# Fetching a 768-word vector as six rows and turning it on TensorE, and loading ScalarE's root table at another place, in a fused attention and gated feed-forward kernel

## The chip, the cores and the metric

The kernel runs on one core of a Trainium2 chip. The time is device microseconds of one execution; before the change the median of four runs is 443.28 us (442.66 to 444.04). A core has five engines, each with its own queue of instructions that it works off in order: TensorE (PE, matmuls; its weight loads, PEld, overlap them), VectorE (DVE), ScalarE (ACT), GpSimd (POOL) and SyncE (SP). They wait for one another by semaphores. DMAs are issued from the queues of SP, ACT and POOL and carried out by 16 DMA engines. ACT evaluates functions from tables; before a function whose table set is not the active one stands an instruction that loads it, ACT_TABLE_LOAD.

## The reference

Eight batches, twelve heads, 448 positions, heads 64 wide. Attention with a squared relu in place of a softmax, then a root-mean-square norm and a gated feed-forward part:

```python
scores = scale * np.matmul(q, k.transpose(0, 1, 3, 2))      # q, k, v: (8, 12, 448, 64) f32
attn = np.maximum(scores, 0.0) ** 2 / S
x = np.matmul(attn, v)                                      # -> (3584, 768)
rms = np.sqrt(np.mean(x * x, axis=-1, keepdims=True) + 1e-06)
xn = x / rms * rms_g                                        # rms_g: (768,)
g = xn @ w_gate                                             # (768, 1536)
silu = g * (1.0 / (1.0 + np.exp(-g)))
return silu * (xn @ w_val) @ w_out                          # (1536, 768), out (3584, 768) f32
```

## The kernel before, in words

Everything is computed in bf16 with f32 sums, one batch at a time, and transposed: x of a batch, `xT`, has the model dimension on the 128 partitions, in six pieces (`KT` = 6) of 448 columns. The norm's weights g must therefore be a column per piece: `ga_sb`, 128 x 6, in which word kt*128 + p of g stands at partition p, column kt, times a constant. `ga_sb` is read wherever a batch's attention output leaves PSUM for `xT` (function `leave`, line 329, on ACT, two pieces at a time; lines 322 and 337 for two pieces of batch 0).

**The order** is the program's order; nothing reorders it. Each engine gets its instructions in the order in which the Python code emits them. `weave` merges a main list (gate and value projections, then output projection tiles) with a list of side steps (attention of the next batch, its norm, fetches), each with a position in the main list.

**The start.** SP fetches the first two heads of k (line 633), ACT those of q, then SP fetches g (line 635) straight into columns. POOL issues the rest. DVE casts the first k (line 648), ACT the first q (649), and DVE makes `ga_sb` from g (line 651). Meanwhile PE does twelve matmuls on zeros (`warm(12)`, line 663). Then the units of `attention_first(0)` follow: unit 0 is `pe_transposes(0, 0)`, sixteen transposes of 112 x 64 into PSUM (line 143), copied out by DVE (line 149); unit 1 is `scores` (line 187), whose relus go to ACT (197) and DVE (195).

**PSUM** has four buffers in the pool `ps_m` (tag "mm"), taken in turn, and two larger ones in `ps_s`.

**The end of a batch's attention.** For batches 1 to 7 the attention output leaves in three pairs of pieces. `leave` of the last pair (pieces 4 and 5) is a side step after the last gate and value block of the batch before; for batches 2 to 7 ACT does two squares (294) and two scaled copies (329) in it, for batch 1 the copies and then one square. Then come two output projection tiles (one for batch 1), whose PSUM ACT copies to `ost` (line 587) and whose store SP issues (602). Then `norm_stat` sums the squares on PE (461), takes the root on ACT (465), loads Silu's table by a one-column Silu (470), takes the reciprocal on DVE (471), spreads it to all partitions (486 on DVE, 488 on ACT), and `norm_apply` multiplies the six pieces by it on DVE (500). After each pair of pieces `swap` copies the halves of the partitions crosswise into `xD` by two DMAs on SP (342). The gate and value projections (`rounds`, line 520) read six pieces of `xT` and six of `xD`, each as a pair of half-height matmuls into psG and psV. Relu, copies and squares between the Silus and the root ask for no table load.

Of the kernel before, what the change touches and what calls it, by code (L numbers as in the profile page):

```python
# [8 lines left out]
FP32 = mybir.dt.float32  # L9
BF16 = mybir.dt.bfloat16  # L10
ALU = mybir.AluOpType
ACT = mybir.ActivationFunctionType
# [17 lines left out]
def along(p0, gap, fns):  # L30
    return [(p0 + gap * i, f) for i, f in enumerate(fns)]
# [3 lines left out]
def kernel(  # L35
# [11 lines left out]
    nc = tc.nc  # L47
    P = nc.NUM_PARTITIONS
# [5 lines left out]
    KT, FT, HP = DM // P, F // P, H // 2  # L54
    assert HP == KT and (2 * S) % P == 0
    eps = 1e-6
    inv_attn = 1.0 / (float(D) * float(S))
# [5 lines left out]
    def pool(name, bufs=1, **kw):  # L63
        return ctx.enter_context(tc.tile_pool(name=name, bufs=bufs, **kw))

    const = pool("consts")
    wpool = pool("weights")
# [6 lines left out]
    ps_m = pool("ps_m", 4, space=bass.MemoryType.PSUM)  # L74
# [4 lines left out]
    def head_rows(t, b, h0, h1):  # L79
        return t[b, h0:h1].rearrange("h (p c) d -> p h (c d)", c=NCH)  # L80
# [12 lines left out]
    def load(nm, b, h0=0, h1=H):  # L93
        src = {"q": q, "k": k, "v": v}[nm]
        return nc.gpsimd.dma_start(out=ld[nm, b][:, h0:h1, :], in_=head_rows(src, b, h0, h1))
# [192 lines left out]
    def leave(b, js):  # L288

        psAV = psAVs.pop((b, js))  # L290
        last = (b, js[0]) == (0, HP - 1)

        def squares_of(i0, i1, o):
            nc.scalar.activation(out=o, in_=psAV[:, i0:i1, :], func=ACT.Square, scale=inv_attn)

        def square():
            if b < 2:
                squares_of(0, len(js), x2s[b][:, js[0] : js[-1] + 1, :])
                return
            t = sums[b]  # L300
            if js[0] == 0:
                squares_of(0, 2, t[:])
                return
            two = npool.tile([P, 2, S], FP32, name="x2f", tag="x2")
            for i in range(2):
                o = two[:, i, :]
                squares_of(i, i + 1, o)
                if js[0] == 2:
                    nc.vector.tensor_tensor(out=t[:, i, :], in0=t[:, i, :], in1=o, op=ALU.add)
                    if i:  # L310
                        nc.vector.tensor_tensor(
                            out=t[:, 0, :], in0=t[:, 0, :], in1=t[:, 1, :], op=ALU.add
                        )
                else:
                    nc.vector.tensor_tensor(out=t[:, 0, :], in0=t[:, 0, :], in1=o, op=ALU.add)

        if last:
            square()
            low, high, every = slice(0, HALF), slice(HALF, P), slice(0, P)
            j = js[0]  # L320
            for dst, to, fr in ((xTs, every, every), (xDs, low, high), (xDs, high, low)):
                nc.vector.tensor_scalar_mul(
                    out=dst[b][to, j, :], in0=psAV[fr, 0, :], scalar1=ga_sb[fr, j : j + 1]
                )
            return
        if b > 1:
            square()
        for i, j in enumerate(js):
            nc.scalar.mul(out=xTs[b][:, j, :], in_=psAV[:, i, :], mul=ga_sb[:, j : j + 1])  # L329
        if b < 2:  # L330
            square()

    def cross(b, j, psAV):

        low, high = slice(0, HALF), slice(HALF, P)
        for to, fr in ((low, high), (high, low)):
            nc.scalar.mul(out=xDs[b][to, j, :], in_=psAV[fr, 0, :], mul=ga_sb[fr, j : j + 1])
# [190 lines left out]
    def early_out(b, fb, parts):  # L528

        t = late["early"].tile([P, 2, S], FP32, name="gv", tag="gv")  # L530
        for part in range(2):
            nc.scalar.copy(out=t[:, part, :], in_=parts[part][:, :S])
        early[fb] = t
# [96 lines left out]
    with fpool as fp:  # L630
        for nm, src, eng in (("k", k, nc.sync), ("q", q, nc.scalar)):
            first[nm] = fp.tile([PC, 2, NCH * D], FP32, name="first_" + nm, tag="first_" + nm)
            eng.dma_start(out=first[nm][:], in_=head_rows(src, 0, 0, 2))
        g_sb = wpool.tile([P, KT], FP32, name="g_sb", tag="rmsg")
        nc.sync.dma_start(out=g_sb[:], in_=moe_rms_g.rearrange("(kt p) -> p kt", p=P))
        load("k", 0, 2, 4)
        load("q", 0, 2, 4)
        ident = const.tile([PC, PC], BF16, name="ident", tag="ident")
        masks.make_identity(nc, ident[:])
        warm_in = const.tile([P, S], BF16, name="warm_in", tag="warm_in")  # L640
        nc.vector.memset(warm_in[:], 0.0)
        ones_bf = const.tile([P, P], BF16, name="ones_bf", tag="ones_bf")
        nc.vector.memset(ones_bf[:], 1.0)
        eps_col = const.tile([P, 1], FP32, name="eps_col", tag="eps_col")
        nc.vector.memset(eps_col[:], eps)
        warm_act = const.tile([P, 1], FP32, name="warm_act", tag="warm_act")
        nc.scalar.activation(out=warm_act[:], in_=eps_col[:], func=ACT.Sqrt)
        nc.vector.tensor_copy(out=ld["k", 0][:, :2, :], in_=first["k"][:])
        nc.scalar.copy(out=ld["q", 0][:, :2, :], in_=first["q"][:])
    ga_sb = wpool.tile([P, KT], FP32, name="ga_sb", tag="rmsga")  # L650
    nc.vector.tensor_scalar_mul(out=ga_sb[:], in0=g_sb[:], scalar1=inv_attn)
    load("k", 0, 4, 6)
    load("q", 0, 4, 6)
    load("v", 0, 0, 6)
    load("k", 0, 6, 12)
    load("q", 0, 6, 12)
    load("v", 0, 6, 12)

    def warm(n):

        ps = ps_m.tile([P, S], FP32, name="psW", tag="mm")
        for _ in range(n):
            nc.tensor.matmul(out=ps[:], lhsT=warm_in[:, :P], rhs=warm_in[:], start=True, stop=True)  # L663
# [16 lines left out]
    def trans_fill(b, half):  # L680
        transposes(b, half)
        fill(b, half, nc.gpsimd)

    with tc.tile_pool(name="qkT", bufs=2, side="right") as tp, tc.tile_pool(
        name="early", bufs=EB, side="right"
    ) as ep:
        late["qkT"], late["early"] = tp, ep
        warm(12)
        steps = attention_second(1)

        def early_block(fb):
            return [ps_m.tile([P, S], FP32, name="psE", tag="mm")[:] for _ in range(2)]

        units = attention_first(0)
        tail = len(units) - 4
        for n, fn in enumerate(units[:tail]):
            fn()
            if n % 3 == 2 and n < tail - 1:
                warm(2)


        raw_x = xTs[0], xDs[0]
        psSS = ps_m.tile([P, S], FP32, name="psSS", tag="mm")
        blocks = [early_block(0)]

        def part(fb, *rs):
            for r in rs:
                rounds(0, fb, blocks[fb], r, r + 1, raw_x)

        psAV4 = psAVs[0, (HP - 2,)]  # L710
        squares_last, leave_4, attend_5, leave_5 = units[tail:]
        squares_last()
        part(0, *range(HP - 2))
        pe_transposes(1, 0)
        leave_4()
        attend_5()
        leave_5()
        cross(0, HP - 2, psAV4)
        part(0, KT, HP - 2, KT + 1, KT + 2)
        norm_stat(0, psSS, steps.pop(0))  # L720
        norm_spread(0)
        blocks.append(early_block(1))
        part(1, *range(KT))
        part(0, HP - 1)
        part(1, *range(KT, KT + 3))
        part(0, KT + 4)
        steps.pop(0)()
        part(1, KT + 4)
        norm_apply(0)
        for fb in range(2):  # L730
            part(fb, KT + 3, KT + 5)
            early_out(0, fb, blocks[fb])
            if fb == 0:
                pe_transposes(1, 1)
        for fb in range(2, EB):
            blocks.append(early_block(fb))
            for r0 in range(0, 2 * KT, KT):
                steps.pop(0)()
                rounds(0, fb, blocks[fb], r0, r0 + KT, raw_x)
            early_out(0, fb, blocks[fb])  # L740
        main = gate_value(0, EB, KT // 2)
        sides = along(6.4, 2, [lambda fb=fb: early_scale(0, fb) for fb in range(EB)])
        sides += along(10.4, 2, [lambda fb=fb: early_rest(0, fb) for fb in range(EB)])
        sides += along(0, (len(main) - 1) / len(steps), steps[:-1])
        sides += [(26, lambda: trans_fill(2, 0))]
        alloc_ld(2)
        load("q", 2)
        load("k", 2)
        for s in range(4, FT // 2):
            fetch_o(s)  # L750
        sides += [(26, lambda: load("v", 2))]
        weave(main, sides)
# [55 lines left out]
```

## Time and profile before

| what | before |
|---|---|
| median of four runs | 443.28 us |
| the profiled execution | 443.27 us, of which span 441.4 us |
| granted TensorE clock, mean | 0.998 |
| PE busy | 432.5 us, 98% |
| ACT busy | 287.6 us, 65% |
| DVE busy | 289.0 us, 65% |
| table loads before the root (L465) | 7 of 1.28 us, 77.8 to 386.4 |
| table loads before the one-column Silu (L470) | 8 of 1.28 us, 34.5 to 388.1 |
| table load before the one-column root at the start (L647) | 1 of 1.28 us, at 1.2 |
| g's transfer (L635) | issued at 1.18, landed 3.9 us later |
| packets under 512 B in the first 8 us | 880 of 2606 |

A line of a timeline has the start in us from the span's beginning, the duration in us, the engine (PEld is PE's weight load; a q behind the name marks its queue, which issues DMAs), the line of the kernel, the operation, what it writes and reads, shapes, how many instructions are merged, and in brackets how long the engine sat idle before it and what it is thought to have waited for. PE's matmuls are pipelined and their ends are modelled: a matmul is drawn with 0.35 us where one starts every 0.19.

### The profile page before, as it was taken

Reading aid. Unit: us, or ns where it says so; the run is one execution under the profiler, and the core shown is the slowest. Engines: PE = TensorE matmul, PEld = TensorE weight load, DVE = VectorE, ACT = ScalarE, POOL = GpSimd, SP = SyncE. Lnnn points to the kernel's source line nnn. Section 1 sums busy time; section 2 is a strip of 40 time slices with the busy share of each in tenths; the row PEclk is TensorE's granted clock in tenths of the full one; section 3 lists DMA queues with packets and bytes.
Section 4 is the critical chain, followed back from the end, with each engine's and each line's share of the span. In section 5 each row is a group of like instructions: output and inputs, shape, how many; then the busy total and the mean of one; then the engine's idle time right before and its main releaser. Section 6 shows DMA issues by size and latency. Waiting matters only on the chain.

```text
span 441.4 us, 10928 instructions
## 1 busy us (share of the span) xinstructions
PE 432.5 (98%) x4718; PEld 248.9 (56%) x4718; DVE 289.0 (65%) x387; ACT 287.6 (65%) x445; POOL 53.7 (12%) x79
## 2 busy tenths in 40 slices
PE   7999999999999999999999999999999999999996
PEld 3445555655566555655566555655557555665564
DVE  4989985777863867766864668578776468742211
ACT  4899886677685775777755776766766677552220
POOL 8333301030001200021000300003000000000000
PEclk9999999999999999999999999999999999999999
DMA  9999999999216991189904996169913900041013
GB/s 146 196 205 198 201 211 188 177 188 153 57 37 148 212 161 29 37 177 168 167 2 105 194 202 85 37 108 198 175 33 75 214 15 1 1 113 59 1 37 109
DMA packets 87632, 53.21 MB, mean 121 GB/s; under 512 B 36768, under 2 KB 83232, under 8 KB 87584
## 3 DMA queue, kind: packets, MB, share of 16 engines
q0 software_dynamic: 44496, 27.50, 43.3%
q1 hardware_dynamic: 42464, 24.44, 27.8%
q8 instruction: 37, 0.61, 0.5%
q10 hardware_dynamic: 624, 0.57, 0.4%
q14 instruction: 11, 0.09, 0.1%
HBM read 47.19 MB, written 11.01 MB: 132 GB/s over the span
## 4 chain that ended last, share of the span: by engine, by line
PE 86%; ACT 7%; DVE 4%; issue 1%; DMA 1%; SPq 0%; ACTq 0%; DVEq 0%
PE psG L520 30%; PE psO L435 23%; PE psV L520 13%; PE psAV L273 9%; PE psS L228 6%; ACT r L217 2%; PE psW L663 2%; DVE r L240 1%; PE psS L187 1%; ACT r L197 1%; ACT sil L564 1%; DVE hT L566 1%; DVE xT L500 1%; DMA xD<-xT 1%; PE psT L143 1%
## 5 line engine op out<-in xcount | busy, mean ns | idle before, releaser
L520 PEld LDWEIGHTS <-wgv_sb 64*128 64x128 bf16 x2304 | 125.2, 94 | 95.5 <-issue 8.1
L520 PE MATMUL psV<-xD,wgv_sb 64*128 64x448 bf16 x558 | 128.4, 349 | 0.3 <-DMA xD<-xT 0.2
L520 PE MATMUL psG<-xD,wgv_sb 64*128 64x448 bf16 x558 | 128.5, 349 | 0.0
L520 PE MATMUL psG<-xT,wgv_sb 64*128 64x448 bf16 x558 | 128.4, 349 | 0.0
L520 PE MATMUL psV<-xT,wgv_sb 64*128 64x448 bf16 x558 | 128.0, 349 | 0.1
L242 ACT ACTIVATE r<-psS 112x896 bf16<-112x896 f32 x108 | 99.1, 918 | 20.5 <-PE psS L228 17.9
L435 PE MATMUL psO<-wo_sb,hT 128*64 128x512 bf16 (+2 forms) x1368 | 111.8, 323 | 0.0
L566 DVE TENSOR_TENSOR hT<-sil,psV 128x448 bf16<-128x448 bf16 x93 | 57.5, 618 | 62.6 <-ACT sil L564 62.4
L246 DVE TENSOR_TENSOR r<-r 112x1792 bf16<-112x1792 bf16 x72 | 78.0, 1088 | 29.2 <-ACT r L242 28.8
L435 PEld LDWEIGHTS <-hT 128*64 128x64 bf16 x1368 | 74.9, 110 | 35.6 <-issue 0.4
L564 ACT ACTIVATE sil<-psG 128x448 bf16<-128x448 f32 x93 | 50.5, 543 | 58.5 <-PE psV L520 35.5
L228 PE MATMUL psS<-qT,kT 64*128 64x448 bf16 (+1 forms) x288 | 56.1, 350 | 0.4
L587 ACT COPY ost<-psO 128x512 f32<-128x512 f32 (+1 forms) x54 | 25.1, 477 | 39.8 <-PE psO L435 39.8
L273 PE MATMUL psAV<-r,vb 112*64 112x448 bf16 x384 | 40.3, 355 | 0.0
L240 DVE TENSOR_SCALAR r<-psS 112x896 bf16<-112x896 f32 x36 | 39.0, 1084 | 1.8 <-PE psS L228 1.8
L175 POOL DMA_DIRECT2D qT<-qT x12 | 6.5, 542 | 264.0 <-PE psS L228 214.3
L273 PEld LDWEIGHTS <-vb 112*64 112x64 bf16 x384 | 20.1, 109 | 18.5 <-issue 6.5
L329 ACT ACTIVATE xT<-psAV,ga_sb 128x448 bf16<-128x448 f32 x47 | 27.8, 646 | 3.9 <-PE psAV L273 3.8
L228 PEld LDWEIGHTS <-kT 64*128 64x128 bf16 (+1 forms) x288 | 19.0, 97 | 16.0 <-issue 4.7
L500 DVE TENSOR_TENSOR xT<-xT,rstd 128x448 bf16<-128x448 bf16 x48 | 26.4, 618 | 2.3 <-ACT rstd L488 2.3
L471 DVE RECIPROCAL rhalf<-rhalf 128x224 f32<-128x224 f32 x8 | 12.4, 1553 | 21.3 <-ACT rhalf L465 21.3
L256 DVE TENSOR_TENSOR r<-r 112x1792 bf16<-112x1792 bf16 x23 | 24.3, 1082 | 0.7 <-ACT r L217 0.7
(68 smaller groups left out, 279.7 us busy)
## 6 DMA issues: line engine op xcount, KB each, us to landing
vb<-in_v_dram POOLq DMA_DIRECT2D x7, 672.0 KB, 18.1
xD<-xT SPq DMA_DIRECT2D x42, 112.0 KB, 2.3
qb<-in_q_dram POOLq DMA_DIRECT2D x6, 672.0 KB, 11.4
kb<-in_k_dram POOLq DMA_DIRECT2D x6, 672.0 KB, 14.4
qT<-qT POOLq DMA_DIRECT2D x24, 168.0 KB, 3.8
out_dram<-ost SPq DMA_DIRECT2D x7, 336.0 KB, 3.9
wgv_sb<-in_moe_w_gate_dram POOLq DMA_DIRECT2D x6, 384.0 KB, 17.5
wgv_sb<-in_moe_w_val_dram POOLq DMA_DIRECT2D x6, 384.0 KB, 17.4
```

The lines of the kernel that those rows point to most:

```text
L228: nc.tensor.matmul(out=psS[: end - o, hf, :S], lhsT=flat[prt, o:end], rhs=qT[prt, 1 - hf : 3 - hf, h % HH], start=True, stop=True,)
L240: nc.vector.tensor_relu(out=r[:, cp], in_=src)
L242: nc.scalar.activation(out=r[:, cp], in_=src, func=ACT.Relu)
L246: nc.vector.tensor_tensor(out=r[:], in0=r[:], in1=r[:], op=ALU.mult)
L273: nc.tensor.matmul(out=part[hh * D : (hh + 1) * D, :], lhsT=ld["v", b][:, 2 * j + hh, c * D : (c + 1) * D], rhs=rsq[b, 2 * j + hh, c], sta ...
L329: nc.scalar.mul(out=xTs[b][:, j, :], in_=psAV[:, i, :], mul=ga_sb[:, j : j + 1])
L435: nc.tensor.matmul(out=ps[prt, :w], lhsT=lhsT[:, prt], rhs=rhs, start=start, stop=stop)
L500: nc.vector.tensor_tensor(out=x[:, kt, :], in0=raw_x[:, kt, :], in1=rstds[b][:], op=ALU.mult)
L520: nc.tensor.matmul(out=parts[part][:, :S], lhsT=wgv_sb[prt, h, fb * P : (fb + 1) * P], rhs=src[prt, kt, :], start=(r == 0), stop=(r == 2 * ...
L564: nc.scalar.activation(out=s[:], in_=psG, func=ACT.Silu)
L566: nc.vector.tensor_tensor(out=hT[:, fb, o : o + S], in0=s[:], in1=psV, op=ALU.mult)
L587: (nc.vector.tensor_copy if last else nc.scalar.copy)(out=osts[i, t][:, o : o + w], in_=ps[:, :w])
```

## The change

Two edits. First, g is fetched as six rows of 128 words, `g_rows`, a row per partition. A 6 x 6 identity in f32 is copied on DVE from the bf16 one. After unit 0, PE transposes `g_rows` into a PSUM tile 128 x 6 of the "mm" buffers, and DVE scales that into `ga_sb`. The scaling at line 651 is gone. Second, for batches 1 to 7 a one-column root is computed on ACT at the end of `leave` of the last pair; since the active table set is Silu's there, the load of the root's set stands in front of this instruction, and the root in `norm_stat` finds its set active.

```diff
@@ leave
         if b < 2:
             square()
+        if b and js[-1] == HP - 1:
+            nc.scalar.activation(out=warm_act[:], in_=eps_col[:], func=ACT.Sqrt)
@@ the start
-        g_sb = wpool.tile([P, KT], FP32, name="g_sb", tag="rmsg")
-        nc.sync.dma_start(out=g_sb[:], in_=moe_rms_g.rearrange("(kt p) -> p kt", p=P))
+        g_rows = wpool.tile([KT, P], FP32, name="g_rows", tag="rmsg")
+        nc.sync.dma_start(out=g_rows[:], in_=moe_rms_g.rearrange("(kt p) -> kt p", p=P))
...
     ga_sb = wpool.tile([P, KT], FP32, name="ga_sb", tag="rmsga")
-    nc.vector.tensor_scalar_mul(out=ga_sb[:], in0=g_sb[:], scalar1=inv_attn)
+    ident_g = const.tile([KT, KT], FP32, name="ident_g", tag="ident_g")
+    nc.vector.tensor_copy(out=ident_g[:], in_=ident[:KT, :KT])
...
+    def columns_of_g():
+
+        psg = ps_m.tile([P, KT], FP32, name="psg", tag="mm")
+        nc.tensor.transpose(out=psg[:], in_=g_rows[:], identity=ident_g[:])
+        nc.vector.tensor_scalar_mul(out=ga_sb[:], in0=psg[:], scalar1=inv_attn)
...
         for n, fn in enumerate(units[:tail]):
             fn()
+            if n == 0:
+                columns_of_g()
             if n % 3 == 2 and n < tail - 1:
                 warm(2)
```

## The prediction, made before the changed kernel was run

> **What bounds the kernel now.** I read the page first: engine totals, the 40 slices, the chain that ended last.
>
> ```profile
> PE 432.5 (98%) x4718; PEld 248.9 (56%) x4718; DVE 289.0 (65%) x387; ACT 287.6 (65%) x445; POOL 53.7 (12%) x79
> ...
> PE   7999999999999999999999999999999999999996
> ...
> PE 86%; ACT 7%; DVE 4%; issue 1%; DMA 1%; SPq 0%; ACTq 0%; DVEq 0%
> ```
>
> TensorE (PE) works from the first slice to the last, and 86% of the chain is its own matmuls. So a shorter wait on another engine is worth time only where a PE instruction is late today, and whatever holds PE's queue back is paid in full. The rest of the reading is a search for both kinds of place, with the timeline of the two stretches that the edit touches. First the start, all engines:
>
> ```profile
> 1.16 4.66 PE L663 MATMUL psW<-warm_in 128*128 128x448 bf16 x12 [1.16 <-DVE warm_in L641]
> 1.18 0.44 SPq L635 DMA_DIRECT2D g_sb<-in_moe_rms_g_dram  x1
> ...
> 4.31 0.57 DVE L648 CAST kb<-first_k 112x512 bf16<-112x512 f32 x1 [3.06 <-DMA first_k<-in_k_dram]
> ...
> 5.09 0.30 DVE L651 TENSOR_SCALAR ga_sb<-g_sb 128x6 f32<-128x6 f32 x1 [0.21 <-DMA g_sb<-in_moe_rms_g_dram]
> ...
> 5.75 0.37 PEld L143 LDWEIGHTS <-kb 112*64 112x64 bf16 x8 [0.73 <-DVE ga_sb L651]
> ...
> 6.13 0.49 PE L143 MATMUL psT<-ident,qb 112*64 112x112 bf16 x8
> ...
> 6.43 0.69 DVE L149 COPY qkT<-psT 128x448 bf16<-128x448 bf16 x2 [1.04 <-PE psT L143]
> ...
> 7.17 0.56 PE L187 MATMUL psS<-qkT 64*128 64x448 bf16 x4 [0.56 <-DVE qkT L149]
> ...
> 7.77 1.09 DVE L195 TENSOR_SCALAR r<-psS 112x896 bf16<-112x896 f32 x1 [0.65 <-PE psS L187]
> ```
>
> The twelve warming matmuls hold PE until 1.16 + 4.66 = 5.82. Then come sixteen transposes, until 6.13 + 0.49 = 6.62, and then PE waits 0.55 us, to 7.17, for VectorE's (DVE's) two copies. DVE in turn is idle between 7.12 and 7.77.
>
> Next the end of a batch's attention, ScalarE (ACT) alone, where batch 3's x leaves:
>
> ```profile
> 178.45 1.20 ACT L329 ACTIVATE xT<-psAV,ga_sb 128x448 bf16<-128x448 f32 x2
> 179.81 0.59 ACT L587 COPY ost<-psO 128x512 f32<-128x512 f32 x1 [0.16 <-PE psO L435]
> 181.12 0.37 ACT L587 COPY ost<-psO 128x256 f32<-128x256 f32 x1 [0.72 <-PE psO L435]
> 181.50 1.28 ACT L465 ACT_TABLE_LOAD   x1
> 182.80 0.45 ACT L465 ACTIVATE rhalf<-psSS,eps_col 128x224 f32<-128x224 f32 x1
> ```
>
> The load stands in front of the root, and ACT idles 0.16 + 0.72 us ahead of it, waiting for the output projection. Last, PE where it first uses the normed and swapped x, for batch 3 and then for batch 7:
>
> ```profile
> 192.22 0.35 PE L520 MATMUL psG<-xD,wgv_sb 64*128 64x448 bf16 x1
> 192.63 0.35 PE L520 MATMUL psV<-xD,wgv_sb 64*128 64x448 bf16 x1
> ...
> 193.02 0.35 PE L520 MATMUL psG<-xD,wgv_sb 64*128 64x448 bf16 x1
> ...
> 193.57 0.35 PE L520 MATMUL psV<-xD,wgv_sb 64*128 64x448 bf16 x1 [0.20 <-DMA xD<-xT]
> ...
> 396.91 0.35 PE L520 MATMUL psG<-xD,wgv_sb 64*128 64x448 bf16 x1
> 397.24 0.35 PE L520 MATMUL psV<-xD,wgv_sb 64*128 64x448 bf16 x1
> ```
>
> Undisturbed, a psG and a psV start together and the next pair 0.19 us later (189.20, 189.39, 189.58). Steps of 0.41 and 0.55 at batch 3, and of 0.33 at batch 7, are waits for a swap's DMA: 0.22 + 0.36 + 0.14 = 0.72 us. The bracket shows only 0.20 of it, because matmuls are drawn overlapping. I found no such step before the xD of batches 2, 4, 5 or 6.
>
> **The start, part by part.** Removed: the 768-word transfer (0.44 us of SP's queue at 1.18, landed 3.9 us later) and DVE's 0.30 us at 5.09. SP's next instruction is a swap at 16.55, so a shorter issue moves nothing; POOL's queue is not touched. The 768 packets leave the rings while the first k and q land, and those could come earlier; but k's cast ends at 4.88 and q's at 4.88 + 0.62 = 5.50, both before PE is through its warming matmuls at 5.82. The gain is 0.
>
> Added on DVE: a 6x6 copy behind k's cast (the 128x1 memset, 0.06 us, is the nearest row) in the 1.04 us of idle time before 6.43; and the scaling, now read from PSUM, behind the two copies. At L651's 0.30 us it runs 7.12 to 7.42 and L195 is not due before 7.77: 0.35 us to spare, and beyond that L195 waits, and PE's scores behind it. ga_sb is first read at 15.89 (ACT L329).
>
> Added on PE: one fp32 transpose of 6 rows, behind the sixteen. No fp32 matmul is in the trace. From below: the sixteen bf16 ones take 0.03 us each in the chain (0.51 us for 16), so it is hidden. From above: the slowest L143 weight load and matmul, 0.18 + 0.30, with a change of tile form before and after at the 0.37 us that the weight loader shows at such changes, 1.22 us, less the 0.55 us of room: 0.67 us late, with scores and everything behind them on PE. A gain is excluded, since the instruction is new. I take 0, by L143, the same operation. It also needs g on chip: 5.09 today behind 768 packets, with 1.5 us to spare before 6.62. Its PSUM buffer is one more turn of the four "mm" ones; of the tiles after it, the first finds the warming tile, which nobody reads, the next two the copied psT, the fourth itself, read by 7.42.
>
> **The table load, part by part.** Seven batches (1 to 7) get one Sqrt of one column behind the last leave: 7 x 0.20 = 1.4 us more on ACT, 65% busy. The loads stay as many; seven of them move from in front of L465 to in front of the new Sqrt. Between the two places ACT has only copies and squares, for which the trace shows no load.
>
> At batch 3: the leave ends at 178.45 + 1.20 = 179.65; load to 180.94, small root to 181.16. Now both copies are due, and two back to back take 0.84 (the row at 185.54): 182.00. psSS is ready (PE's four L461 end at 181.27), so L465 runs from 182.02 instead of 182.80: 0.78 us earlier. Behind it Silu's load, the reciprocal, the spread, DVE's six L500 and the six swaps follow in the same order, all 0.78 earlier if the DMAs are as long. The last swap landed at 193.53 and would at 192.75; the psV that wants it would, with the earlier 0.22 regained, be due at 192.80. So both steps vanish, and by the same offsets batch 7's: 0.72 us. At batch 1 the order is leave to 76.61, load, small root to 78.10, one copy to 78.71: L465 0.42 us earlier, where no PE step is late.
>
> What is queued behind the moved load: the first copy, from 179.81 to 181.17 (1.36 us later), and the second, some 0.5. A copy frees a PSUM buffer. The first projection tile's is next wanted four tiles on, after psO2, psSS and psO3: 181.27 + 2.6 (two thirds of the 3.92 us for 48 matmuls) = 183.9, against 181.76 when it is free; 2.1 us to spare. Without it, each us of delay would be one of PE. On SP the output store waits for the second copy and is issued 0.5 us later, at 182.0 for 0.79; the swaps behind it, at 186.85 - 0.78 = 186.07, are not reached. No DMA is issued from ACT in between.
>
> One rule speaks against the move. The Trainium skill, ScalarE: Activation LUTs, section "What ACT_TABLE_LOAD costs", puts every switch at about 2.66 us, a drain of some 1.38 included. The trace shows the next activation 1.30 us after the load began (181.50, 182.80), and no drain. By the page the root at batch 3 would start at 179.65 + 2.66 + 0.20 + 0.84 = 183.35, some 0.55 later than today, and that estimate, paid at batches 3 and 7, makes 444.4 us.
>
> **The sum** is made against the profiled execution's own 443.27 us (span 441.4 and 1.87 around it; the median of the runs shown is 443.28): 443.27 - 0.72 + 0 = 442.55. From 57.4 to the end PE shows no other wait above 0.1 us, and its small waits on DVE's relus (0.07 us, six times) hang on PE's own earlier work, so a gain at 193 is kept.
>
> **The rivals.**
> *Nothing to gain at the swaps.* Four of the six comparable batches show no late xD with the same offsets. At batch 3 the last swap's issue held SP 1.37 us instead of 0.57, and its landing took 3.24 us where others' median is 2.2. Batch 5 shows a 1.38 too, unhurt. If that is chance, or follows the swap wherever it goes, 0 to 0.14 is gained: 443.1 to 443.3. Against it: the profiled execution is as long as the median, and an earlier swap helps at any length.
> *The turn of g holds PE (the other side).* The transpose stands in PE's queue ahead of all scores. If g lands late, every 0.1 us past 6.6 costs 0.1. It eats the 0.72 when the transpose ends past 7.9 and makes the kernel slower by 0.9 when past 8.8. The transfers issued in the first 8 us landed after 3.5 to 8.1 us; at 8.1 g comes at 9.3, PE resumes at about 9.5, +2.3 - 0.72: 444.9. Against it: that one is 336 KB on POOL's queue; g is 3 KB and today's slower form needs 3.9.
> *More is gained.* The wait list says that the first weight load waited 0.73 for DVE's ga_sb, which the change takes away. At the warming matmuls' pace it could come at 5.24, 0.51 sooner: 442.04. Against it: that load reads only kb, which was cast at 4.88, and after every warming pair the next form's weights come 0.07 us before the pair's drawn end, as here (5.75, 5.82).
>
> **How the numbers follow.** A measurement of this kernel can tell about 0.2%, 0.89 us, from no change: 442.4 to 444.2 is "same". Swaps gained 0.50; nothing gained 0.25; more gained 0.13; PE held at the start 0.12, of which 0.08 past 444.2. The likeliest, 442.55, is inside the band but 0.16 from its edge, so 0.10 of its share ends beyond: with 0.13 that makes 0.23 faster, 0.08 slower, 0.69 same. The range goes from 442.04 to the nothing-gained case with the transpose's upper bound, 443.27 + 0.67 = 443.94, and 0.15 beyond both for the median's own spread (the runs shown lie 0.6 and 0.8 about theirs): 441.9 to 444.1.
>
> **What would show it.** Right: seven ACT_TABLE_LOADs behind the last leave and none in front of L465; at batch 3 the root at about 182.0; a psG to psV step of 0.19 where 0.41, 0.55 and 0.33 stood; PE's first scores still at 7.17. Wrong: scores later than 7.3, a psO matmul that waits for a copy, a load followed by an idle ACT, or a step of 0.4 still there with the swaps earlier.

## The result and the profile after

The changed kernel takes 442.46 us (median of 37 runs, 441.64 to 443.18) against 443.37 us (58 runs) for the kernel before: a ratio of 0.9979, interval 0.9975 to 0.9984, so 0.7 to 1.1 us faster. The profiled execution took 442.53 us, its span 440.7. The page says little: PE is as busy, its share of the chain that ended last is up from 86% to 89%, and no DMA stands in that chain any more. Nearly all of the 771 packets fewer are g's words.

```profile
PE 432.2 (98%) x4719; PEld 248.9 (56%) x4719; DVE 289.0 (66%) x388; ACT 287.4 (65%) x452; POOL 53.7 (12%) x79
...
DMA packets 86861, 53.22 MB, mean 121 GB/s; under 512 B 35990, under 2 KB 82460, under 8 KB 86812
...
PE 89%; ACT 7%; DVE 3%; issue 1%; DVEq 0%
```

The start, all engines (start, duration, engine, line; lines from 333 on are two or more higher than before):

```profile
1.16 4.66 PE L672 MATMUL psW<-warm_in 128*128 128x448 bf16 x12 [1.16 <-DVE warm_in L643]
...
1.19 0.38 SPq L637 DMA_DIRECT2D g_rows<-in_moe_rms_g_dram  x1
...
4.79 0.15 DVE L654 CAST ident_g<-ident 6x6 f32<-6x6 bf16 x1
...
5.75 0.37 PEld L143 LDWEIGHTS <-kb 112*64 112x64 bf16 x8 [0.73 <-issue]
...
6.64 0.16 PEld L665 LDWEIGHTS psg<-ident_g,g_rows 6*128 6x128 f32 x1
6.64 0.25 PE L665 MATMUL psg<-ident_g,g_rows 6*128 6x6 f32 x1
...
7.06 0.15 DVE L666 TENSOR_SCALAR ga_sb<-psg 128x6 f32<-128x6 f32 x1
7.20 0.56 PE L187 MATMUL psS<-qkT 64*128 64x448 bf16 x4 [0.31 <-DVE qkT L149]
```

The turn of g sits in the room between the transposes and the first scores: PE's idle time before them fell from 0.56 to 0.31 us and they start at 7.20 instead of 7.17. The first weight load comes at 5.75 as before, although no ga_sb is made ahead of it. ACT's cast of q began at 4.56 instead of 4.88, which nobody used.

ACT at the end of batch 3's attention:

```profile
178.38 1.20 ACT L329 ACTIVATE xT<-psAV,ga_sb 128x448 bf16<-128x448 f32 x2
179.58 1.28 ACT L333 ACT_TABLE_LOAD   x1
180.87 0.20 ACT L333 ACTIVATE warm_act<-eps_col 128x1 f32<-128x1 f32 x1
180.98 0.84 ACT L589 COPY ost<-psO 128x512 f32<-128x512 f32 x2
181.71 0.46 ACT L467 ACTIVATE rhalf<-psSS,eps_col 128x224 f32<-128x224 f32 x1
```

The load follows the leave without a gap, both copies run back to back, and the root starts 2.13 us after the leave's end instead of 3.15 (179.65 to 182.80): 1.02 us earlier. PE where it first uses the swapped x of batch 3, and of batch 7:

```profile
192.16 0.35 PE L522 MATMUL psG<-xD,wgv_sb 64*128 64x448 bf16 x1
192.16 0.35 PE L522 MATMUL psV<-xD,wgv_sb 64*128 64x448 bf16 x1
...
192.73 0.35 PE L522 MATMUL psG<-xD,wgv_sb 64*128 64x448 bf16 x1
192.73 0.35 PE L522 MATMUL psV<-xD,wgv_sb 64*128 64x448 bf16 x1
...
396.21 0.35 PE L522 MATMUL psG<-xD,wgv_sb 64*128 64x448 bf16 x1
396.21 0.35 PE L522 MATMUL psV<-xD,wgv_sb 64*128 64x448 bf16 x1
```

psG and psV of each pair start together: the steps of 0.41 and 0.55 are gone, and so is the 0.33 of batch 7 (the pair at 396.21).

### The profile page after: what moved, and what is told of

It reads as the page before. It is cut to its first block, busy times and chain, and to the rows that moved or that the text cites. A ratio compares the mean times of both kernels' runs of the same rounds, so it can differ in the third digit from the quotient of the medians.

```text
span 440.7 us, 10936 instructions
## 1 busy us (share of the span) xinstructions
PE 432.2 (98%) x4719; PEld 248.9 (56%) x4719; DVE 289.0 (66%) x388; ACT 287.4 (65%) x452; POOL 53.7 (12%) x79
## 4 chain that ended last, share of the span: by engine, by line
PE 89%; ACT 7%; DVE 3%; issue 1%; DVEq 0%
PE psG L522 31%; PE psO L437 25%; PE psV L522 13%; PE psAV L273 9%; PE psS L228 6%; ACT r L217 2%; PE psW L672 2%; DVE r L240 1%; PE psS L187 1%; ACT r L197 1%; ACT sil L566 1%; DVE hT L568 1%; PE psT L143 1%; PE psS L207 1%; ACT qkT L151 1%
## 5 line engine op out<-in xcount | busy, mean ns | idle before, releaser
L522 PEld LDWEIGHTS <-wgv_sb 64*128 64x128 bf16 x2304 | 124.9, 94 | 94.9 <-issue 7.4
L522 PE MATMUL psG<-xT,wgv_sb 64*128 64x448 bf16 x558 | 128.4, 349 | 0.0
L522 PE MATMUL psV<-xD,wgv_sb 64*128 64x448 bf16 x558 | 128.1, 349 | 0.0
L522 PE MATMUL psV<-xT,wgv_sb 64*128 64x448 bf16 x558 | 128.0, 349 | 0.1
L522 PE MATMUL psG<-xD,wgv_sb 64*128 64x448 bf16 x558 | 128.1, 349 | 0.0
```

The costliest lines, as they stand in the source:

```text
L522: nc.tensor.matmul(out=parts[part][:, :S], lhsT=wgv_sb[prt, h, fb * P : (fb + 1) * P], rhs=src[prt, kt, :], start=(r == 0), stop=(r == 2 * ...
```

## Experiments

Runs of one group share a chip and its runs of the kernel before.

### Which half, and which batch

`g_only` leaves the small root out, `root_only` takes nothing else of the change. The other two have the whole change, with the small root for some batches:

```diff
-        if b and js[-1] == HP - 1:
+        if b in (3, 7) and js[-1] == HP - 1:            # root_3_7
+        if b in (1, 2, 4, 5, 6) and js[-1] == HP - 1:   # root_others
             nc.scalar.activation(out=warm_act[:], in_=eps_col[:], func=ACT.Sqrt)
```

> The change with its first half alone: g as six rows turned by PE, no small root behind the leave. Theory (the gain is the late swaps of batches 3 and 7, reached through the root): no gain, within 0.1 us of the kernel before, and the steps of 0.41, 0.55 and 0.33 between psG and psV still stand. Rival (the 0.2 us that the medians moved beyond the 0.7 between the two profiles, or more, comes from the start): 0.2 to 0.5 us faster.

> The second half alone: the small root behind the last leave, g still by 768 words. Theory: the whole gain, 0.7 to 0.9 us, and the three steps gone. Rival (both halves needed, or the start pays): at most 0.5 us.

> The whole change, but the small root only for batches 3 and 7, where a psV was late. Theory: the whole gain, 0.7 to 0.9 us. Rival (each of the seven moved loads is worth some 0.1 us): 2 of 7, about 0.25 us.

> The whole change, but the small root for batches 1, 2, 4, 5 and 6 alone. Theory: nothing, within 0.1 us of the kernel before, with the steps at batches 3 and 7 as before. Rival (each moved load counts): 5 of 7, about 0.65 us.

| run | median us (before 443.3) | ratio, interval |
|---|---|---|
| g_only | 443.42 | 1.0001, 0.9992 to 1.0010 |
| root_only | 442.66 | 0.9983, 0.9974 to 0.9992 |
| root_3_7 | 442.08 | 0.9974, 0.9962 to 0.9985 |
| root_others | 443.42 | 0.9999, 0.9990 to 1.0008 |

The new way of fetching g is worth nothing that can be measured. The moved load is the gain, and of its seven places two carry it: the other five (`root_others`) leave the time where it was. In `root_others` PE still waits at batch 3:

```profile
192.35 0.35 PE L522 MATMUL psG<-xD,wgv_sb 64*128 64x448 bf16 x1
193.01 0.35 PE L522 MATMUL psV<-xD,wgv_sb 64*128 64x448 bf16 x1 [0.31 <-DMA xD<-xT]
...
193.40 0.35 PE L522 MATMUL psG<-xD,wgv_sb 64*128 64x448 bf16 x1
193.94 0.35 PE L522 MATMUL psV<-xD,wgv_sb 64*128 64x448 bf16 x1 [0.18 <-DMA xD<-xT]
```

Over the pace of 0.19 these steps lose 0.47 + 0.35, and batch 7's 0.14. In `g_only` it is 0.14 + 0.33 + 0.12. In `root_only` and `root_3_7` none is left. That `root_3_7` came out below the other kernels with those two loads moved is within its interval, and I make nothing of it.

### The same mechanism turned round, and by half

`root_thrice` is the kernel before with the root of batches 1 to 7 computed three times into the same place, so later. `moved_half` is the changed kernel with the root of batches 3 and 7 computed twice.

```diff
-        nc.scalar.activation(
-            out=half[:], in_=psSS, func=ACT.Sqrt, scale=1.0 / float(DM), bias=eps_col[:]
-        )
+        for _ in range(3 if b else 1):             # root_thrice; moved_half: 2 if b in (3, 7) else 1
+            nc.scalar.activation(
+                out=half[:], in_=psSS, func=ACT.Sqrt, scale=1.0 / float(DM), bias=eps_col[:]
+            )
```

> The kernel before, with the root of batches 1 to 7 computed three times in a row into the same place, which makes it some 0.8 us later (two of 0.45 us, overlapping a little). Theory: paid where the last swap is late or nearly so. Batches 3 and 7 pay all of it; batch 5, whose last swap I estimate to land 0.6 us ahead of its psV (issued at 292.7, 2.2 us to landing, wanted at 295.5), pays 0.2; the others, with 3 us and more, nothing: 1.8 us slower, 1.4 to 2.1. Rival (ACT's time is what counts, whichever batch): 7 times 0.8, over 5 us. Rival (the norm is covered): 0.

> The changed kernel with the root of batches 3 and 7 computed twice, so that there it is only 0.3 us earlier than in the kernel before instead of 0.8. Theory by lateness alone (the last swap of batch 3 began too late, and each tenth counts): at batch 3 the last swap lands at 193.2 where its psV is due at 192.8, so 0.3 to 0.4 us of the 0.7 remain; batch 7's 0.14 is gained: 0.35 to 0.45 us faster than before. Rival (it is a collision: in every trace without the earlier root the last swap of batch 3 held SP for 1.3 to 1.7 us, in every trace with it 0.6; any shift that avoids it gains all): as fast as the changed kernel, with a longest issue of 0.6.

`root_thrice`: 445.66 against 443.45 us, ratio 1.0049, 1.0027 to 1.0072, so 1.2 to 3.2 us slower. The three roots took 1.41 us, and the swaps of batch 3 began 8.17 us after the leave's end instead of 7.20: 0.97 later, not 0.8. PE in that trace, at batches 3, 5 and 7:

```profile
192.04 0.35 PE L521 MATMUL psG<-xD,wgv_sb 64*128 64x448 bf16 x1
193.50 0.35 PE L521 MATMUL psV<-xD,wgv_sb 64*128 64x448 bf16 x1 [1.10 <-DMA xD<-xT]
...
193.89 0.35 PE L521 MATMUL psG<-xD,wgv_sb 64*128 64x448 bf16 x1
194.45 0.35 PE L521 MATMUL psV<-xD,wgv_sb 64*128 64x448 bf16 x1 [0.21 <-DMA xD<-xT]
...
296.42 0.35 PE L521 MATMUL psG<-xD,wgv_sb 64*128 64x448 bf16 x1
296.94 0.35 PE L521 MATMUL psV<-xD,wgv_sb 64*128 64x448 bf16 x1 [0.17 <-DMA xD<-xT]
...
398.06 0.36 PE L521 MATMUL psG<-xD,wgv_sb 64*128 64x448 bf16 x1
398.24 0.35 PE L521 MATMUL psV<-xD,wgv_sb 64*128 64x448 bf16 x1
398.73 0.35 PE L521 MATMUL psG<-xD,wgv_sb 64*128 64x448 bf16 x1
399.39 0.35 PE L521 MATMUL psV<-xD,wgv_sb 64*128 64x448 bf16 x1 [0.31 <-DMA xD<-xT]
```

Batch 3 loses 1.27 + 0.37 = 1.64 (0.58 before), and batch 5 for the first time 0.33. Batch 7 loses 0.07 at a step that is not shown, 0.48 where the psG at 398.73 comes 0.67 after the last one, and 0.47 at the psV behind it: 1.02 (0.14 before). That makes 2.3 us more, and nothing at batches 1, 2, 4 and 6. The median of 2.2 us lies above the 1.4 to 2.1 expected, because the swaps came 0.97 later and not 0.8. Lateness is paid where the slack is used up and nowhere else. Both rivals, all seven batches or none, fall.

`moved_half`: 442.69 against 443.15 us, ratio 0.9987, 0.9978 to 0.9995; `after_again` in the same group 0.9986, 0.9977 to 0.9995. The times do not tell the two apart, and both intervals hold the 0.35 to 0.45 us expected. By the trace the swaps of batch 3 began 6.68 us after the leave's end, so 0.52 earlier than before and not 0.3; of the 0.58 us, 0.06 should then remain, and one step of 0.32, 0.13 over the pace, does:

```profile
192.07 0.35 PE L523 MATMUL psG<-xD,wgv_sb 64*128 64x448 bf16 x1
192.39 0.35 PE L523 MATMUL psV<-xD,wgv_sb 64*128 64x448 bf16 x1
```

Here is how long SP was held by each of the six swaps of batch 3 (least, median, longest, in ns) in the kernel before, the changed one and `moved_half`:

```profile
L342 SPq DMA_DIRECT2D xD<-xT x6: 477/554/1373, 186.9 to 190.3; - x6
```

```profile
L344 SPq DMA_DIRECT2D xD<-xT x6: 471/560/598, 185.8 to 189.2; - x6
```

```profile
L344 SPq DMA_DIRECT2D xD<-xT x6: 472/556/1471, 185.6 to 189.0; - x6
```

The long issue is still there in `moved_half`, and hurts little. Nor does it lengthen the transfer: the last swap of batch 3 landed 3.2 us after its issue began in the kernel before and in the changed one alike. So the gain does not come from avoiding the long issue; the swaps being earlier is enough. But it is no chance event: it is 1.29 to 1.84 us in `g_only`, `root_others`, `root_thrice` and `before_warm_10` too, and 0.60 at most in every trace with the whole shift. A 16 KB packet of an instruction queue goes with it: in the kernel before, it starts at 190.23 and takes 1.11 us, and the last swap is issued at 190.30. In all six traces with the long issue such a packet starts at most 0.07 us ahead of that swap's issue, and in the other eight only as the issue ends, or later. That this packet is the cause was not tested.

> The changed kernel itself, beside the three others of this call on one chip: 0.7 to 1.1 us faster than the kernel before.

442.38 against 443.15 us: 0.2 to 1.0 us faster, which overlaps with what was expected and lies a little lower.

### The start

`turn_8` repeats the transposition of g, `warm_10` and `before_warm_10` change one number:

```diff
-        nc.tensor.transpose(out=psg[:], in_=g_rows[:], identity=ident_g[:])
+        for _ in range(8):                                                # turn_8
+            nc.tensor.transpose(out=psg[:], in_=g_rows[:], identity=ident_g[:])
...
-        warm(12)
+        warm(10)                                                          # warm_10, before_warm_10
```

> The changed kernel with the transposition of g done eight times in a row into the same tile. One took 0.25 us as drawn, and the scores came 0.03 us later than before. Theory (whatever holds PE's queue at the start is paid in full once the room before the scores, 0.3 us, is used): seven more at 0.1 to 0.25 us each, 0.4 to 1.4 us later at the first scores, and as much slower at the end than the changed kernel, so 0.5 us faster to 0.5 us slower than the kernel before. Rival (the start has slack further on, by 57 us): as fast as the changed kernel, 0.9 us faster than before, although the first scores come later.

> The changed kernel with ten warming matmuls for twelve. Theory (the first transposes wait for the warming matmuls and for nothing else): PE is free 0.75 us earlier; k's cast ends at 4.87 and q's at 5.18, so the transposes of k begin at 5.0 and the scores at about 6.5, and 0.3 to 0.7 us is gained on the changed kernel (1.2 to 1.6 on the one before). Rival (the clock opens later for want of work, and the scores run slow): no gain, or a loss of up to 0.5 us.

> The kernel before with ten warming matmuls for twelve. g's 768 words are still in the way of q, whose cast ended at 5.50, and DVE's scaling, which waits for them until 5.09, stands ahead of the copies. Theory: the transposes of q begin at 5.55, the scores at about 6.6; 0.2 to 0.6 us faster than before, so some 0.1 to 0.2 us less than the same edit brings the changed kernel. Rival (g's form doesn't matter here either): the same gain as in the changed kernel within 0.05 us.

| run | median us (before 443.45) | ratio, interval |
|---|---|---|
| turn_8 | 442.60 | 0.9980, 0.9969 to 0.9991 |
| warm_10 | 442.58 | 0.9986, 0.9967 to 1.0005 |
| before_warm_10 | 443.20 | 0.9994, 0.9982 to 1.0006 |

The intervals of `warm_10` and `before_warm_10` both hold 1, so the two don't tell whether g's form matters with ten warming matmuls.

`turn_8` missed its purpose. Eight turns took 0.66 us where one takes 0.25, so one more costs 0.06, and all eight fit into the room. PE was not held: the turns ended at 6.86, as DVE's copies did, and the scores began at 6.91. The rule that a held PE is paid in full was not tested by it.

In `warm_10` the scores did start earlier, at 6.43, and the gain was eaten by 29 us: the first psE matmul (batch 0's first gate and value projections) came at 29.36 instead of 28.97. PE's waits between 4 and 32 us (engine, line, what it waited for, total, times, longest) show where:

```profile
PE psS L187 <- ACT r L197: 1.5, 3, 0.8
PE psT L143 <- DMA qb<-in_q_dram: 0.8, 1, 0.8
PE psS L187 <- DVE qkT L149: 0.3, 1, 0.3
PE psAV L273 <- DMA vb<-in_v_dram: 0.3, 1, 0.3
```

The waits for ACT and for `qkT` stand in the changed kernel too; those for q and v are new. The transfers of q's and v's next heads are a second bound, close behind the warming matmuls. Where it lies differs between executions: `before_warm_10` (scores at 6.41) waits 0.6 us for the same q, `g_only` (6.31) not at all. So I split these transfers, with twelve and with ten warming matmuls:

```diff
-    load("v", 0, 0, 6)
-    load("k", 0, 6, 12)
-    load("q", 0, 6, 12)
+    load("v", 0, 0, 2)
+    load("k", 0, 6, 8)
+    load("q", 0, 6, 8)
+    load("v", 0, 2, 6)
+    load("k", 0, 8, 12)
+    load("q", 0, 8, 12)
     load("v", 0, 6, 12)
```

> The changed kernel with ten warming matmuls, and with batch 0's transfers in another order: v of two heads, then k and q of two heads, then v of four, k, q and v of the rest, instead of six heads each at a time. Theory (with ten warming matmuls the start ran into v's and q's second transfers, 0.3 and 0.8 us of waits, and that alone ate the 0.75): no wait for a transfer of batch 0, and 0.5 to 0.75 us faster than the changed kernel, 1.3 to 1.7 faster than the one before. Rival (the rings are full and something else comes late instead): no faster than the changed kernel.

> The changed kernel with the new order of transfers alone, twelve warming matmuls. Theory (PE starts at a fixed work, transfers only cut the executions in which the clock opened early): 0 to 0.3 us faster than the changed kernel. Rival: the two more issues on POOL delay the weights and it is slower.

`split_12` took 442.57 us, ratio 0.9984, 0.9975 to 0.9993, the same as the changed kernel beside it. `split_10` took 443.08, ratio 1.0000, 0.9982 to 1.0019, with single runs from 441.45 to 446.18. Its trace has no wait for a transfer of batch 0, as expected, but something else:

```profile
1.16 3.92 PE L675 MATMUL psW<-warm_in 128*128 128x448 bf16 x10 [1.16 <-DVE warm_in L643]
...
8.44 0.93 PE L675 MATMUL psW<-warm_in 128*128 128x448 bf16 x2
...
11.68 0.55 PE L675 MATMUL psW<-warm_in 128*128 128x448 bf16 x2
```

Two warming matmuls take 0.93 us at 8.4 and 0.55 at 11.7: PE ran at its slow pace until about 10 us in this execution. The clock records of its trace turn to the full clock at 10.0 us; in the two other traces with ten warming matmuls they do at 5.4 and 5.5, in the eleven with twelve at 3.8 to 7.2. The transfers are not all; with ten warming matmuls the fast pace can come late. No version here beats the changed kernel by more than the noise.

## Why the prediction was right

The prediction, 442.55 us, was 0.1 us above what was measured, and the sign, the mechanism and the range held. By its steps:

- **The start costs and gains 0.** Right. `g_only` is at 1.0001. The turn took 0.25 us as drawn against the bounds of 0.03 and 1.22; the scaling from PSUM took 0.15, not 0.30, the 6x6 copy 0.15, not 0.06.
- **The room was never filled.** The rival in which the turn holds PE needed it to end past 7.9; it ended at 6.89. (That rival was sized too small: of the transfers issued in the first 8 us, the last landed after 11.0 us, not 8.1.) The rival in which the ga_sb of the wait list frees PE is refuted by the load at 5.75 in the changed kernel, with no ga_sb ahead of it, and by `warm_10`, where the same load moved to 5.00 with the warming matmuls.
- **The root at batch 3 0.78 us earlier.** It was 1.02. The term that failed is the small root and the two copies taken as 0.20 and 0.84 in a row: the first copy began 0.11 us after the small root did, and the root 0.73 us after the copies did, since neighbouring ACT instructions overlap as drawn. It did not matter, because PE had only 0.58 to gain there.
- **0.22 + 0.36 + 0.14 us of late psV.** All three steps went, and `root_3_7` and `root_others` show that these two batches hold the gain.
- **No PSUM buffer comes free too late behind the delayed copies.** Right: the first copy began 1.17 us later (180.98 for 179.81) and no psO matmul waited.
- **The rule that spoke against the move.** Between the load's begin and the next activation are 1.29 us (179.58, 180.87), and in all 14 profiles the next activation begins 0.01 us after each load's end. The drain that the Trainium skill, ScalarE: Activation LUTs, section "What ACT_TABLE_LOAD costs", adds would have made the change a loss by the estimate on record; the measurement decides against it here. That estimate was also lopsided: it put the page's price on the moved load and the measured one on the load of today.
- **The sum.** 0.72 was forecast and 0.91 (0.7 to 1.1) measured. The steps differ between executions: 0.72 in the profiled one of the kernel before, 0.59 in `g_only`, 0.96 in `root_others`. The clearest measure is from PE's first scores to the start of DVE's last copy of the output, which leaves out the start's chance and the last stores':

| kernel | first scores | last copy | between |
|---|---|---|---|
| before | 7.17 | 437.54 | 430.37 |
| g_only | 6.31 | 436.53 | 430.22 |
| root_others | 7.18 | 437.88 | 430.70 |
| after | 7.20 | 436.69 | 429.49 |
| after_again | 7.19 | 436.68 | 429.49 |
| split_12 | 7.17 | 436.65 | 429.48 |
| turn_8 | 6.91 | 436.42 | 429.51 |
| root_only | 6.49 | 436.04 | 429.55 |
| root_3_7 | 6.56 | 436.18 | 429.62 |

Without the load moved at batches 3 and 7 the mean is 430.43, with it 429.52: 0.91 us. To place it, each weight load of the gate and value projections (L520, L522) can be set against the same one in the profile before. The changed kernel gains 0.61 us at batch 3, 0.14 at batch 7 and 0.06 at batch 1: 0.81 of the 0.86 that it gains between the first of these loads and the last. The 0.06 was not in the sum: a scores matmul that starts at 97.47 in the kernel before starts at 97.40. This delay stands in `g_only`, `before_warm_10` and `root_3_7` too, and is gone in every profile in which batch 1's root comes at another time, earlier or, in `root_thrice`, later. Why is open.

- **Nothing to gain at the swaps**, the rival given one in four, was wrong, and `root_thrice` shows why its argument was weak: that four batches show no wait says that they have slack, not that lateness is free. The long landing at batch 3 was no chance either: it stayed at 3.2 us and came earlier with its swap. The other issue of 1.38 us that the rival names is batch 4's (236.6 to 240.5), not batch 5's.

## What to carry to other kernels

A load of a function table, or any work that needs no input, belongs ahead of a wait and not behind it; but look which consumer is late before counting it, since here two of seven places paid and the sum of seven loads said nothing. Waits of paired, overlapped matmuls are understated by idle time (0.20 us listed against 0.58 lost); the step between starts against the undisturbed pace gives their price. And when the start of a kernel varies by more than the effect, compare the distance between two fixed events of the trace.

## What the runs showed that was not expected

Executions of the same work differ at the start. The twelve warming matmuls took 4.66 us in the profiles of the kernel before and after, 3.99 in that of `g_only` and 3.74 in that of `moved_half`:

```profile
1.16 3.99 PE L670 MATMUL psW<-warm_in 128*128 128x448 bf16 x12 [1.16 <-DVE warm_in L641]
```

```profile
1.16 3.74 PE L673 MATMUL psW<-warm_in 128*128 128x448 bf16 x12 [1.16 <-DVE warm_in L644]
```

At first one starts every 0.37 us, later every 0.19 (in `moved_half` at 3.37, 3.75, 3.97, 4.16). The traces' clock records agree: they turn to the full clock at 3.8 us in `moved_half`, at 4.3 in `g_only`, at 6.4 in the kernel before and at 6.7 in the changed one. The mean granted clock of a page counts the time ahead of this record as full.

The first scores came at 6.30 to 7.20, and this difference is carried to the last copy, as the table shows (after and `root_only` are 0.71 apart at the start and 0.65 at the end). The Trainium skill, TensorE: Matmul & The Clock Gate, section "What's actually happening", says that the window in which PE's activity is judged runs freely and does not start with the kernel, so that the change of pace moves by ±500 ns from run to run. The traces agree that it moves, and by more: the full clock begins between 3.8 and 7.2 us in the eleven profiles with twelve warming matmuls. Less is carried where the second bound is met: `moved_half`, first scores at 6.30, waited 0.3 us for q's second transfer, and `root_thrice`, at 6.69, 0.4 us. From the start of the last copy another 3.8 to 4.8 us pass until the span ends, by how the last stores land (440.0 - 436.18 in `moved_half`, 440.8 - 436.04 in `root_only`).
